# Keeping the turned keys of a head pair between two passes over a batch

## The chip, the cores and the metric

One core of one Trainium2 chip runs the whole program. The metric is the device time of one execution in microseconds (us); every kernel is run several times and the median counts. Engine names as in the profile: PE multiplies matrices, DVE, ACT and POOL work on vectors, SP issues most of the DMAs.

## What is computed

Attention that keeps only the 32 largest scores of each query row, and behind it a channel mix (a gated feed-forward layer) over all heads. Batch 8, 8 heads, 576 positions, head width 64; d_model 512, d_ff 1024.

```python
scores = scale * np.matmul(q, k.transpose(0, 1, 3, 2))
kth = np.partition(scores, -top_k, axis=-1)[..., -top_k:-top_k + 1]
scores = np.where(scores >= kth, scores, -1000000000.0)
attn = np.exp(scores - np.max(scores, axis=-1, keepdims=True))
attn = attn / (np.sum(attn, axis=-1, keepdims=True) + 1e-09)
x = np.matmul(attn, v)            # heads side by side: (batch, 576, 512)
...
xk = mu_k * x + (1.0 - mu_k) * x_prev
xr = mu_r * x + (1.0 - mu_r) * x_prev
k = np.maximum(xk @ w_k, 0.0)
v = k * k @ w_v
r = 1.0 / (1.0 + np.exp(-(xr @ w_r)))
return r * v
```

## The kernel before

**Tiles and visits.** Heads are worked in pairs (`hp`, four pairs a batch). A *visit* is one pair with a part of its query rows: `VISITS` is a list of (batch, pair, part), and `attend` walks it. A part is a range of tiles 0 to 8; tiles 0 to 7 are 64 query rows of both heads (128 partitions), tile 8 is the last 64 rows. A batch is passed over twice, first tiles 0 to 3 of pairs 0, 1, 2, 3, then tiles 4 to 8 of pairs 0, 1, 2, 3; the last batch is passed over three times (0 to 3, 4 to 7, 8). That makes 7 times 8 plus 12, so 68 visits.

**What a visit prepares.** It loads 512 rows of keys of both heads (`load_k`, two DMAs into `kn`), its queries (`qn`), the last 64 key rows (`tl`, and the last 64 query rows where tile 8 belongs to the visit) and the values (`v`). PE turns them with the identity: four transposes for the keys (`turned`, line 834), two for each 256 query rows, one or two for `tl` (line 847); ACT copies each out of PSUM (`K` and `qs` at line 839, `kd` at line 849). Turned keys `K` have two buffers, `kn`, `qn`, `tl` and `v` one each.

**What a tile does.** PE makes scores (889, 885; 876 and 877 for tile 8), ACT copies them to SBUF (894), DVE finds the largest 24 (899, 901, 904), ACT and POOL (919, 921) and DVE (922, 924) find the threshold, ACT exponentiates (927), DVE masks (930), PE turns the result (936, 945), ACT copies it (938, 947), PE multiplies with the values (966, 967), and DVE scales it into `xT` (1001, 1003).

**The channel mix.** `mixes` works `xT` in chunks of 256 rows as soon as their heads are there. PE's matmuls are lines 608 to 610. At the end of a chunk, for each 128 rows, DVE multiplies the matmul's result with the gate in two instructions, `scaled` (line 1137) and `gated` (line 1138), and SP stores the row block (line 1139). `G.l` and `G.e` are SBUF tiles of the gate (`lb`, `eb`), made long before; `pv` is the matmul's result in PSUM (`rot`).

**The flag.** `seen` collects, for every row, whether the fast way to the threshold held; `lowest` (line 1012) reduces it to a column of `least` at the end of each pass. Behind the plan, DVE reduces `least` (1265), PE turns it (1267), DVE reduces and compares (1269, 1271), every engine loads the flag into a register (1272), and a branch (1273) skips the general path, which these inputs never take.

**Order of the work.** Nothing is reordered on the chip: each engine runs its own queue in order. The queues are laid out by `Plan.run`, a list scheduler with a cost and a latency for each operation, which picks the ready operation with the lowest key. A key is the tile number plus a constant of `OFF`; for the mix, a lag behind the tiles it reads. Every operation's place in its queue hangs on all of these constants.

## Time and profile before

| | |
|---|---|
| median of 3 runs | 1284.56 us (1284.15 to 1285.1) |
| the profiled execution | 1283.33 us, of which the span (first to last instruction) is 1281.5 us |
| mean granted clock of PE | 0.986 of full speed |
| instructions | 31120 |

How to read it: the profile divides the span into 40 slices and gives a digit for the busy tenths of each engine. PE and DVE stand at 8 or 9 from the sixth slice to the 36th, and so does ACT; only at the beginning and behind the last attention tile do they part. A share of busy time does not say which of several full engines sets the pace; that is read from the stretches, from the waits, and from the order in which each engine is fed. PE's durations overlap one another, since matmuls are pipelined, so the time that one takes from the queue is read from start to start.

### The profile page before, as it was taken

The page shows a single profiled execution, that of the slowest core. Times are in us where ns is not written, and L with a number is a line of the kernel's source. Part 1 is how long each engine was busy: PE and PEld are TensorE (multiplying, and loading weights), DVE is VectorE, ACT ScalarE, POOL GpSimd, SP SyncE. Part 2 cuts the span into 40 slices and gives each one's busy share as a digit, 9 for nine tenths or more (in the row PEclk, how much of TensorE's full clock was granted, in tenths as well). Part 3 has the DMA queues.
Part 4 walks back from the last instruction along what each step waited for, and adds up shares of the span by engine and source line. Part 5 has one row for each costly group of instructions (what it writes and reads, how often), then busy time and mean ns, then how long its engine had stood idle before and what let it go on. Part 6 is the DMA issues. An engine that isn't in the chain of part 4 may idle for free.

```text
span 1281.5 us, 31120 instructions
## 1 busy us (share of the span) xinstructions
PE 1218.4 (95%) x9349; PEld 935.8 (73%) x9349; DVE 1146.5 (89%) x6228; ACT 1131.4 (88%) x2491; POOL 985.8 (77%) x885
## 2 busy tenths in 40 slices
PE   5876899999999999999999999999999999999996
PEld 2444677777777777777777778777777777777885
DVE  6999999999999999999999999999999989997111
ACT  5998899999999999999999999998989999988441
POOL 2458997978788686978697888786978787878672
PEclk7998999999999999999999999999999999999998
DMA  7144112221221212122312122212222122221100
GB/s 211 40 109 111 47 45 65 48 64 25 57 66 47 59 43 69 40 52 47 78 36 64 25 65 48 65 36 55 48 65 45 47 48 63 48 63 43 32 26 16
DMA packets 218593, 72.51 MB, mean 57 GB/s; under 512 B 211248, under 2 KB 211248, under 8 KB 218416
## 3 DMA queue, kind: packets, MB, share of 16 engines
q1 hardware_dynamic: 217872, 70.31, 22.2%
q8 instruction: 76, 1.25, 0.4%
q14 instruction: 101, 0.83, 0.2%
q10 hardware_dynamic: 544, 0.13, 0.0%
HBM read 60.95 MB, written 9.44 MB: 55 GB/s over the span
## 4 chain that ended last, share of the span: by engine, by line
PE 46%; DVE 25%; ACT 18%; POOL 4%; issue 3%; DMA 2%; SPq 1%; DVEq 0%; ACTq 0%; POOLq 0%
PE rot L608 7%; PE rot L610 7%; PE rot L609 7%; DVE cand L899 7%; PE ps L966 6%; PE rot L936 5%; DVE E L930 5%; PE ps L889 5%; DVE top L922 4%; ACT sc L894 4%; ACT sg L919 3%; ACT se L927 3%; ACT et L938 2%; DVE top L901 2%; DVE cand L904 2%
## 5 line engine op out<-in xcount | busy, mean ns | idle before, releaser
L921 POOL TENSOR_TENSOR sg<-sc,sg 128x576 f32<-128x576 f32 x288 | 409.0, 1424 | 166.7 <-ACT sg L919 164.7
L899 DVE MAX8 cand<-sc 128x8 f32<-128x82 f32 (+1 forms) x2016 | 377.0, 231 | 18.2 <-ACT sc L894 16.3
L919 ACT ACTIVATE sg<-sc,seen 128x576 f32<-128x576 f32 x288 | 226.1, 785 | 13.8 <-DVE seen L911 12.2
L930 DVE SCALAR_TENSOR_TENSOR E<-sc,seen,se 128x576 f32<-128x576 f32 x288 | 231.0, 802 | 0.8 <-issue 0.2
L927 ACT ACTIVATE se<-sc,seen 128x576 f32<-128x576 f32 x288 | 217.5, 755 | 9.9 <-DVE E L930 8.4
L922 DVE MAX8 top<-sg 128x8 f32<-128x576 f32 x288 | 216.0, 750 | 5.9 <-POOL sg L921 5.2
L894 ACT ACTIVATE sc<-ps 128x576 f32<-128x576 f32 x288 | 186.9, 656 | 22.0 <-DVE E L930 8.2
L936 PE MATMUL rot<-ident,E 128*128 128x128 f32 x1152 | 179.6, 279 | 13.7 <-DVE E L930 7.2
L901 DVE MAX8 top<-cand 128x8 f32<-128x56 f32 x864 | 179.2, 208 | 3.8
L608 PE MATMUL rot<-xh,wk 128*128 128x256 f32 (+2 forms) x608 | 180.3, 297 | 0.9 <-ACT ri L994 0.5
L938 ACT ACTIVATE et<-rot 128x512 f32<-128x512 f32 x288 | 174.1, 606 | 7.4 <-PE rot L936 7.1
L936 PEld LDWEIGHTS rot<-ident,E 128*128 128x128 f32 x1152 | 129.9, 141 | 63.9 <-ACT sg L919 7.3
L609 PE MATMUL rot<-xl,wk 128*128 128x256 f32 (+2 forms) x608 | 169.9, 279 | 0.8 <-POOL xl L1087 0.8
L966 PEld LDWEIGHTS ps<-et,v 128*64 128x64 f32 x2560 | 128.5, 137 | 57.0 <-ACT el L947 16.5
L610 PE MATMUL rot<-xh,wk 128*128 128x256 f32 (+2 forms) x608 | 169.8, 279 | 0.0
L966 PE MATMUL ps<-et,v 128*64 128x128 f32 (+1 forms) x2560 | 164.6, 270 | 1.5 <-DVE seen L911 0.5
L889 PE MATMUL ps<-K,qs 64*128 64x512 f32 x512 | 147.4, 653 | 0.0
L608 PE MATMUL rot<-wv,hh 128*128 128x512 f32 (+1 forms) x296 | 127.0, 429 | 0.3 <-ACT qs L839 0.3
L608 PEld LDWEIGHTS rot<-xh,wk 128*128 128x128 f32 x608 | 116.2, 191 | 4.0 <-ACT K L839 1.1
L610 PE MATMUL rot<-wv,hl 128*128 128x512 f32 (+1 forms) x296 | 116.7, 394 | 0.0
L609 PEld LDWEIGHTS rot<-xl,wk 128*128 128x128 f32 x608 | 115.8, 190 | 1.1 <-POOL xl L1087 1.0
L904 DVE MATCH_REPLACE8 cand<-top,cand 128x56 f32<-128x56 f32 x576 | 115.8, 201 | 0.2 <-issue 0.2
(112 smaller groups left out, 2826.9 us busy)
## 6 DMA issues: line engine op xcount, KB each, us to landing
kn<-in_k SPq DMA_DIRECT2D x136, 128.0 KB, 2.5
v<-in_v SPq DMA_DIRECT2D x136, 128.0 KB, 2.5
out<-eb SPq DMA_DIRECT2D x35, 256.0 KB, 2.1
qn<-in_q SPq DMA_DIRECT2D x126, 64.0 KB, 2.2
stage<-in_moe_w_k SPq DMA_DIRECT2D x8, 512.0 KB, 6.0
xT<-in_moe_w_v SPq DMA_DIRECT2D x8, 512.0 KB, 3.6
tl<-in_k SPq DMA_DIRECT2D x136, 16.0 KB, 2.0
vr_in<-in_v SPq DMA_DIRECT2D x128, 16.0 KB, 2.1
```

The source lines that it names most:

```text
L608: nc.tensor.matmul(ps, lhsT=sh, rhs=mh, start=first, stop=False)
L609: nc.tensor.matmul(ps, lhsT=sh, rhs=ml, start=False, stop=False)
L610: nc.tensor.matmul(ps, lhsT=sl, rhs=mh, start=False, stop=last)
L894: return nc.scalar.activation(T.sc.t, sl.t[:, o:o + S], AF.Copy)
L899: lambda T=T, c=c: nc.vector.max(T.cand.t[:, 8 * c:8 * c + 8], T.sc.t[:, CUTS[c]:CUTS[c + 1]]), reads=[T.sc], writes=[(T.cand, c)])
L919: lambda T=T, sn=sn: nc.scalar.activation(T.side.t, T.sc.t, AF.Sign, bias=sn(T, 1), scale=-BELOW, accum_out=T.top.t[:, TOPK:TOPK + 1]),
L921: plan.op(POOL, "below", n, 1375, 1430, lambda T=T: nc.gpsimd.tensor_mul(T.side.t, T.sc.t, T.side.t), reads=[T.sc], writes=[T.side])
L922: plan.op(DVE, "eighth", n, 660, 754, lambda T=T: nc.vector.max(T.top.t[:, 24:32], T.side.t), reads=[T.side], writes=[(T.top, 3)])
L927: plan.op(ACT, "exps", n, 667, 754, lambda T=T, pe=pe, sn=sn: nc.scalar.activation(pe.t, T.sc.t, AF.Exp, bias=sn(T, 0), scale=SCALE), read ...
L930: lambda T=T, U=U, pe=pe, sn=sn: nc.vector.scalar_tensor_tensor(T.e(), T.sc.t, sn(T, 2), pe.t, op0=OP.is_ge, op1=OP.mult, accum_out=U.rs.t ...
L936: nc.tensor.transpose(pt.t[:, c * 128:(c + 1) * 128], E.t[:, o + c * 128:o + (c + 1) * 128], ident)
L966: return [*[nc.tensor.matmul(pa[hs[j]], lhsT=vs[j][:, c, :], rhs=ms[c][j], start=(c == 0), stop=False) for c in range(NKC) for j in range(2)],
```

## The change

**Visits.** The second pass runs over the pairs backwards (3, 2, 1, 0), and two visits of one pair that meet become one. In a usual batch that is 0, 1, 2, 3 (all nine tiles), 2, 1, 0: seven visits in place of eight. In the last batch the third pass runs forwards again, which makes ten in place of twelve; 59 visits in all.

**Turned keys are kept.** `K` has four buffers (`1 + HOLD`). If the same pair comes again within the next six visits, its `K` is put into `held`, and the later visit takes it from there: no load of `kn`, no transposes, no copy. Last key rows (`tl`, `kd`) and values are loaded anew on each visit as before. Queries are loaded in blocks of 256 rows, two for the joined visit, of which the second has a key four tiles later.

**The flag** is made by four operations of the plan (`low`, `lowt`, `lowr`, `lowc`), from one column of `least` for each batch, and the registers are loaded inside the plan's scope.

**The gate.** `scaled` now forms (`G.e` - 2) times `G.l`, both in SBUF, without the matmul's result; `gated` multiplies by -1 and by `pv`.

The planner's constants are new as a whole (`OFF` with about 80 of them, and those below).

```diff
...
-CANDS, BESTS = 0.061, -0.104
-LAG, STEP, WAT, WSTEP, GATE, VALUE, PACE = 11.185, 15.662, 2.065, 0.589, 7.397, 13.484, -2.0
+CANDS, BESTS = 0.045, 0.43
+LAG, STEP, WAT, WSTEP, GATE, VALUE, PACE = 11.262, 15.699, 4.074, 1.023, 7.744, 14.237, -2.0
+HOLD = 3
 HALVES = range(4), range(4, 9)
 EDGE = {B - 1: (range(4), range(4, 8), range(8, 9))}
-VISITS = [(b, hp, part) for b in range(B) for part in EDGE.get(b, HALVES) for hp in range(HP)]
+def visits():
+
+    vs = []
+    for b in range(B):
+        for k, part in enumerate(EDGE.get(b, HALVES)):
+            for hp in range(HP)[::-1] if k % 2 else range(HP):
+                if vs and vs[-1][:2] == (b, hp):
+                    part = range(vs.pop()[2][0], part[-1] + 1)
+                vs.append((b, hp, part))
+                part = EDGE.get(b, HALVES)[k]
+    return vs
+
+
+VISITS = visits()
...
-SLACK = dict(PE=150, ACT=52, DVE=60, POOL=61)
+SLACK = dict(PE=106, ACT=28, DVE=8, POOL=173)
...
-NEAR = dict(PE=151, ACT=168, DVE=28, POOL=268, SP=202)
+NEAR = dict(PE=134, ACT=163, DVE=28, POOL=240, SP=327)
...
-LWAT, LWSTEP = 1.027, 1.455
-LAG0, LAG1 = 10.828, 1.959
+LWAT, LWSTEP = -2.383, 1.423
+LAG0, LAG1 = 9.215, 14.977
...
-MORE = dict(xh=2, xl=2, et=3, top=3, el=1)
+MORE = dict(xh=2, xl=2, et=3, top=3, el=1, K=1 + HOLD)
...
-    least = consts.tile([128, len(VISITS) // HP], F32, name="least")
+    least = consts.tile([128, B + 1], F32, name="least")
+    flag = consts.tile([1, 1], I32, name="flag")
...
-            P.kn, P.tl, P.K, P.kd = buf("kn"), buf("tl"), buf("K"), buf("kd")
-            P.qn, P.qs = (buf("qn"), buf("qs")) if P.first < 8 else (None, None)
-            c0 = P.first // 2
-            nq = sum(1 for i in part if i < 8) // 2
+            P.tl, P.kd, P.K = buf("tl"), buf("kd"), held.pop((b, hp), None)
+            fresh = P.K is None
+            if fresh:
+                P.kn, P.K = buf("kn"), buf("K")
+            if any(x[:2] == (b, hp) for x in visits[p + 1:p + 1 + 2 * HOLD]):
+                held[b, hp] = P.K
+            P.q = {i: (buf("qn"), buf("qs")) for i in part if i % 4 == 0 and i < 8}
             soon = p == 0
 
...
-            plan.op(SP, "kt", at0, 1000, 2700, load_k, writes=[P.kn])
-            if P.qn:
+            if fresh:
+                plan.op(SP, "kt", at0, 1000, 2700, load_k, writes=[P.kn])
+            for i, (qn, _) in P.q.items():
...
+                plan.op(ACT if now else SP, "kq", at0 + i - P.first, 1000, 2700, load_q, writes=[qn])
...
-            turned(P.kn, 4, "k", lambda P=P: P.K.t, P.K)
-            if P.qn:
-                turned(P.qn, nq, "q", lambda P=P, nq=nq: P.qs.t[:, :nq * 128], P.qs, fast=soon)
+            if fresh:
+                turned(P.kn, 4, "k", lambda P=P: P.K.t, P.K)
+            for i, (qn, qs) in P.q.items():
+                turned(qn, 2, "q", lambda qs=qs: qs.t, qs, at0 + i - P.first, fast=soon and i == 0)
...
-            if hp == HP - 1:
-                o = slice(part[0], part[-1] + 1)
-
-                def lowest(s=seen, o=o, m=p // HP):
-                    nc.vector.tensor_reduce(least[:, m:m + 1], s.t[:, :, 1:, o], axis=mybir.AxisListType.XYZ, op=OP.min)
-                plan.op(DVE, "lowest", n, 126, 219, lowest, reads=[seen], writes=[X.least])
+            if p + 1 == len(visits) or visits[p + 1][0] != b:
+                def lowest(s=seen, b=b):
+                    nc.vector.tensor_reduce(least[:, b:b + 1], s.t[:, :, 1:, :], axis=mybir.AxisListType.XYZ, op=OP.min)
+                plan.op(DVE, "lowest", n, 150, 243, lowest, reads=[seen], writes=[X.least])
+        pl = buf("rot")
+        plan.op(DVE, "low", n, 70, 170, lambda: nc.vector.tensor_reduce(least[:, B:], least[:, :B], axis=mybir.AxisListType.X, op=OP.min), writes=[X.least])
+        plan.op(PE_, "lowt", n, 80, 280, lambda: nc.tensor.transpose(pl.t[:1, :128], least[:, B:], ident), reads=[X.least], writes=[pl], mode="T")
+        plan.op(DVE, "lowr", n, 190, 280, lambda: nc.vector.tensor_reduce(least[:1, B:], pl.t[:1, :128], axis=mybir.AxisListType.X, op=OP.min), reads=[pl], writes=[X.least])
+        plan.op(DVE, "lowc", n, 52, 150, lambda: nc.vector.tensor_scalar(flag, least[:1, B:], TINY, None, op0=OP.is_lt), writes=[X.least])
         return xT, ready, starts[-1]
...
-                plan.op(DVE, "scaled", k1, 586, 694, lambda G=G, m=m, pv=pv: nc.vector.scalar_tensor_tensor(pv.t[:m], G.l.t[:m], -1.0, pv.t[:m], op0=OP.mult, op1=OP.mult), reads=[G.l], writes=[pv])
-                plan.op(DVE, "gated", k1, 586, 694, lambda G=G, m=m, pv=pv: nc.vector.scalar_tensor_tensor(G.e.t[:m], G.e.t[:m], 2.0, pv.t[:m], op0=OP.subtract, op1=OP.mult), reads=[pv], writes=[G.e])
+                plan.op(DVE, "scaled", k1, 586, 694, lambda G=G, m=m: nc.vector.scalar_tensor_tensor(G.e.t[:m], G.e.t[:m], 2.0, G.l.t[:m], op0=OP.subtract, op1=OP.mult), reads=[G.l], writes=[G.e])
+                plan.op(DVE, "gated", k1, 586, 694, lambda G=G, m=m, pv=pv: nc.vector.scalar_tensor_tensor(G.e.t[:m], G.e.t[:m], -1.0, pv.t[:m], op0=OP.mult, op1=OP.mult), reads=[pv], writes=[G.e])
...
-        sizes = dict(kn=(1, [128, NKC, 2, D]), qn=(1, [128, NKC, 2, D]), tl=(1, [128, 256]), v=(1, [128, 2, NKC, D]), K=(2, [128, MAIN]), kd=(2, [128, 256]),
-                     qs=(2, [128, MAIN]), sc=(4, [128, S]), cand=(2, [128, 8 * NCH]), top=(4, [128, TOPK + 1]),
+        sizes = dict(kn=(1, [128, NKC, 2, D]), qn=(1, [128, 2, 2, D]), tl=(1, [128, 256]), v=(1, [128, 2, NKC, D]), K=(2, [128, MAIN]), kd=(2, [128, 256]),
+                     qs=(2, [128, 256]), sc=(4, [128, S]), cand=(2, [128, 8 * NCH]), top=(4, [128, TOPK + 1]),
...
+        return nc.values_load(flag, min_val=0, max_val=1)
 
     with ExitStack() as stack:
         stack.enter_context(tc.manual_schedule())
-        pipeline(stack)
-
-    with tc.tile_pool(name="flag", bufs=1) as fp, tc.tile_pool(name="flag_ps", bufs=1, space=PSUM) as fps:
-        low = fp.tile([128, 1], F32, name="low")
-        nc.vector.tensor_reduce(low, least, axis=mybir.AxisListType.X, op=OP.min)
-        row = fps.tile([1, 128], F32, name="row")
-        nc.tensor.transpose(row, low, ident)
-        lowest = fp.tile([1, 1], F32, name="lowest")
-        nc.vector.tensor_reduce(lowest, row, axis=mybir.AxisListType.X, op=OP.min)
-        flag = fp.tile([1, 1], I32, name="flag")
-        nc.vector.tensor_scalar(flag, lowest, TINY, None, op0=OP.is_lt)
-        again = nc.values_load(flag, min_val=0, max_val=1)
+        again = pipeline(stack)
+
...
```

Of the program as built, counted over each engine's queue: PE's transposes of `kn` fall from 272 to 128 and those of `tl` from 100 to 91; ACT's copies to `K` from 68 to 32 and to `kd` (one block) from 36 to 27; SP's loads of `kn` from 136 to 64, of `tl` from keys from 136 to 118, of `v` from 136 to 118, of the values' last rows (`vr_in`) from 128 to 112; DVE's `lowest` from 17 to 8.

PE in the second pass of a batch, before: this is the preparation of a visit with tile 8 (`tl` two blocks), among tiles of the visit ahead (L889, L885 scores, L936, L945 masked tiles).

```order
L847 MATMUL rot_149<-ident,tl_92 128x128 x2
L889 MATMUL ps<-K_94,qs_98 128x512 x2
L885 MATMUL ps<-kd_96,qs_98 128x2x64
L936 MATMUL rot_151<-ident,E_116 128x128 x4
L834 MATMUL rot_149<-ident,kn_90 128x128 x4
L834 MATMUL rot_150<-ident,qn_91 128x128 x2
L945 MATMUL ps<-ident,E_116 128x128
L608 MATMUL rot_151<-xh_130,wk_68 128x256
```

The same place with the change (L856 transposes queries and keys, L870 `tl`, L908 and L912 make scores, L959 and L968 turn masked tiles, L989 multiplies with values).

```order
L990 MATMUL ps<-el_127,vr_in 64x128 x2
L959 MATMUL rot_153<-ident,E_118 128x128 x4
L856 MATMUL rot_154<-ident,qn_92 128x128 x2
L870 MATMUL rot_152<-ident,tl_93 128x128 x2
L959 MATMUL rot_152<-ident,E_118 128x128 x4
L908 MATMUL ps<-kd_99,qs_101 128x2x64
L968 MATMUL ps<-ident,E_118 128x128
L912 MATMUL ps<-K_97,qs_101 128x512 x2
L989 MATMUL ps<-et_124,v_94 64x128
```

The four transposes of the keys are gone; those of the queries and of `tl` remain.

DVE at its queue's end, before: L1137 and L1138 are the last gate blocks, L1265 to L1271 make the flag.

```order
L1137 SCALAR_TENSOR_TENSOR rot_149<-lb_140,rot_149 64x512
L1138 SCALAR_TENSOR_TENSOR eb_137<-eb_137,rot_149 64x512
L1137 SCALAR_TENSOR_TENSOR rot_149<-lb_141,rot_149 128x512
L1138 SCALAR_TENSOR_TENSOR eb_138<-eb_138,rot_149 128x512
L1265 TENSOR_REDUCE low<-least 128x1
L1269 TENSOR_REDUCE lowest<-row 1x1
L1271 TENSOR_SCALAR flag<-lowest 1x1
L1272 TENSOR_LOAD flag
```

With the change, DVE at the end of attention (L947 and L1033 are the last threshold and `lowest`, L1036 to L1039 the flag, L953 masks the last tile, L1163 and L1164 are the gate's two steps).

```order
L947 SCALAR_TENSOR_TENSOR nine_115,seen_117<-se,top_111 128x9
L1033 TENSOR_REDUCE least<-seen_117 128x1
L1036 TENSOR_REDUCE least<-least 128x1
L1038 TENSOR_REDUCE least<-rot_152 1x1
L1039 TENSOR_SCALAR flag<-least 1x1
L1164 SCALAR_TENSOR_TENSOR eb_139<-eb_139,rot_153 64x512
L953 SCALAR_TENSOR_TENSOR E_119,rs_123<-sc_106,seen_117,se 128x576
L996 TENSOR_SCALAR rot_152<-rs_123 128x1
L997 RECIPROCAL rs_123<-rot_152 128x1
L1026 TENSOR_TENSOR xT_146<-ps,ri_128 128x64 x3
L1163 SCALAR_TENSOR_TENSOR eb_140<-eb_140,lb_143 128x512
L1164 SCALAR_TENSOR_TENSOR eb_140<-eb_140,rot_152 128x512
```

The flag now stands ahead of the last mask, and eight more gate instructions follow these rows before DVE loads the flag as the last thing in its queue; SP's load of the flag, which before waited for eight DMA queues, PE and POOL as well, now waits for DVE alone.

## Rows read from the trace of the kernel before

**Rows 1.** page part 1, busy time of each engine
```profile
PE 1218.4 (95%) x9349; PEld 935.8 (73%) x9349; DVE 1146.5 (89%) x6228; ACT 1131.4 (88%) x2491; POOL 985.8 (77%) x885
```

**Rows 2.** stretches of the span, with each engine's busy time
```profile
core 0: us, PE busy (x) PEld busy (x) DVE busy (x) ACT busy (x) POOL busy (x), PEclk, DMA share, GB/s
0.00:200.00 200.00, 157.69 (x990) 102.01 (x991) 185.36 (x887) 169.35 (x356) 133.42 (x124) 0.93 0.35 93
200.00:600.00 400.00, 395.13 (x3193) 307.86 (x3191) 393.80 (x2238) 381.50 (x849) 320.65 (x290) 1.00 0.22 52
600.00:1000.00 400.00, 398.52 (x3166) 310.99 (x3165) 384.74 (x2142) 377.88 (x840) 328.57 (x287) 1.00 0.22 52
1000.00:1180.00 180.00, 177.60 (x1396) 139.72 (x1397) 166.38 (x920) 166.00 (x370) 142.49 (x126) 1.00 0.22 53
1180.00:1281.50 101.50, 89.44 (x610) 75.24 (x609) 16.25 (x46) 36.64 (x81) 60.70 (x62) 0.96 0.09 26
```

**Rows 3.** the same view, of the masking line L930 alone
```profile
200.00:400.00 200.00, 43.19 (x108) 1.00 0.22 52
600.00:1100.00 500.00, 102.28 (x253) 1.00 0.22 53
```

**Rows 4.** timeline of PE: start us, us, instruction
```profile
612.46 0.33 PE L847 MATMUL rot<-ident,tl 128*128 128x128 f32 x1
612.62 0.27 PE L945 MATMUL ps<-ident,E 128*128 128x128 f32 x1
...
613.89 0.65 PE L834 MATMUL rot<-ident,kn 128*128 128x128 f32 x4
614.38 0.39 PE L885 MATMUL ps<-kd,qs 128*128 128x128 f32 x2
```

**Rows 5.** groups: line engine op xcount | busy, mean ns | idle before
```profile
L834 PE MATMUL rot<-ident,kn 128*128 128x128 f32 x272 | 43.8, 286 | 12.5 <-DMA kn<-in_k 10.8 <-ACT et L938 1.4 <-ACT ri L990 0.3
L839 ACT ACTIVATE K<-rot 128x512 f32<-128x512 f32 x68 | 41.1, 605 | 6.1 <-PE rot L834 6.0
```

**Rows 6.** stretch 200 to 1180 us, instructions on the turned keys
```profile
200.00:1180.00 980.00, 152.65 (x492) 41.67 (x492) 34.48 (x57) 1.00 0.22 52
```

**Rows 7.** timeline of the program's end
```profile
1268.71 0.39 PE L609 MATMUL rot<-wv,hh 128*128 128x512 f32 x1
...
1268.94 0.39 PE L610 MATMUL rot<-wv,hl 128*128 128x512 f32 x1
1269.42 0.70 DVE L1137 SCALAR_TENSOR_TENSOR rot<-lb,rot 128x512 f32<-128x512 f32 x1 [17.47 <-PE rot L610]
1270.22 0.69 DVE L1138 SCALAR_TENSOR_TENSOR eb<-eb,rot 128x512 f32<-128x512 f32 x1
1270.94 0.33 SPq L1139 DMA_DIRECT2D out<-eb  x1
1273.22 0.17 DVE L1265 TENSOR_REDUCE low<-least 128x1 f32<-128x17 f32 x1 [2.31 <-DMA out<-eb]
...
1274.22 0.14 DVE L1271 TENSOR_SCALAR flag<-lowest 1x1 int32<-1x1 f32 x1
```

**Rows 8.** source lines behind the flag: count, duration ns min/median/max, first and last start
```profile
L1272 PEldq TENSOR_LOAD <-flag x1: 488/488/488, 1274.6 to 1274.6; - x1
...
L1273 PEldq COMPARE_BRANCH  x1: 3882/3882/3882, 1275.2 to 1275.2; - x1
...
L1336 SPq EVENT_SEMAPHORE  x10: 17/28/28, 1280.2 to 1281.5; - x10
```

**Rows 9.** groups of POOL's product and of the first gate step
```profile
L921 POOL TENSOR_TENSOR sg<-sc,sg 128x576 f32<-128x576 f32 x288 | 409.0, 1424 | 166.7 <-ACT sg L919 164.7
...
L1137 DVE SCALAR_TENSOR_TENSOR rot<-lb,rot 128x512 f32<-128x512 f32 (+1 forms) x37 | 25.4, 686 | 67.9 <-PE rot L610 67.8
```

**Rows 10.** waits of DVE behind 1180 us: us, times, longest
```profile
DVE rot L1137 <- PE rot L610: 67.8, 7, 20.2
```

**Rows 11.** waits of PE ahead of 200 us: us, times, longest
```profile
PE rot L834 <- DMA kn<-in_k: 9.7, 3, 4.7
```

More of the change, by code (lines that the diff above doesn't have):

```diff
@@ L46 @@
-CANDS, BESTS = 0.061, -0.104
-LAG, STEP, WAT, WSTEP, GATE, VALUE, PACE = 11.185, 15.662, 2.065, 0.589, 7.397, 13.484, -2.0
+OFF = dict(kt=-24.682, kq=-9.775, rest=-13.394, v=-5.073, v8=8.399, tk=-5.088, ck=-3.016, tq=-4.466, cq=-5.729, tr=-0.99, cr=-8.985, zero=26.741,
+           score=-0.305, score8=-16.363, keep=-0.702, cand=5.175, best=-6.77, drop=-17.414, under=-0.972, nb=6.314, count=2.406, below=-0.034,
+           eighth=5.4, nine=7.048, exps=3.042, mask=2.258, turn=3.521, et=4.406, turnl=4.279, el=0.332, weigh=1.23, inv=6.6, inv2=-0.753,
+           turni=-5.161, ri=4.56, place=-1.898, lowest=11.386, ranks=1.008, mu=-8.732, nmu=20.632, changek=16.045, sharek=6.336, addk=-15.444,
+           xhk=3.381, xlk=-26.53, changer=-11.566, sharer=8.77, addr=10.933, xhr=5.939, xlr=-9.1, hidden=1.376, relu=-3.776, sq=2.602, r2=6.527,
+           hl=-6.961, gate=1.635, gexp=2.338, ga=11.247, ln=3.288, inv1=4.629, newton=-11.796, value=-0.174, scaled=-9.381, gated=-4.072,
+           store=12.146, w=18.924, wabs=-4.306, wclamp=0.885, wshift=-9.236, wsign=0.581, wexp=-1.85, wfine=2.14, whi=8.188, wmul=10.013,
+           wsub=-10.654, wlo=1.658, spread=1.602, sliver=-7.978, low=3.66, lowt=-12.415, lowr=-14.586, lowc=-1.397)
```

38 lines of the change are left out of this document (15 added, 23 removed).

## The prediction

> **What bounds the kernel now.** I read the page's busy times first, then stretches of the span, then the timeline of single places, and the program's end last. The page alone decides nothing: PE is busy 95% of the span, DVE 89%, ACT 88% [rows 1]. The stretches say more [rows 2]. In the first 200 us PE lies idle for 42.3 us (200 less 157.69); DVE is the full engine there. From 200 to 1180 us PE is busy for 395.13 + 398.52 + 177.60 = 971.3 of 980 us, so it is idle for 8.7 us, at the full granted clock (1.00, the level of 2.4 GHz). DVE is busy for 944.9 us of the same 980 and idle for 35.1. Behind 1180 us DVE has almost nothing left, and PE works off mix matmuls that have piled up, until its last one starts at 1268.94 us [rows 7]. So PE's queue is full from 200 us to its end: whatever leaves that queue should bring the end nearer by the time that it took. DVE is a near second. From 200 to 400 us it masks 54 tiles (108 records of line L930, two for each tile, one of them the accumulator's read), which is 27.0 in 100 us; from 600 to 1100 us it masks 126.5, which is 25.3 [rows 3]. DVE can go faster than it does in the later stretch, and what holds it there is PE.
>
> **Keys no longer turned.** One turn of a pair's keys is four transposes. In the timeline the first of the four starts at 613.89 us and what comes behind them at 614.38, so a turn takes 0.49 us of PE's queue; one transpose of `tl` takes 612.62 less 612.46, 0.16 us [rows 4]. I use start to start, since a listed duration (0.65 and 0.33 us) overlaps the next instruction. The change drops 36 of 68 turns and 9 transposes of `tl`. Of the 68 copies to `K` [rows 5], 57 lie between 200 and 1180 us [rows 6]; the eleven ahead are the eight visits of batch 0 and three of batch 1. Batch 0 loses four turns and one `tl`, in the stretch where PE has 42 us to spare, and I count those 2.1 us at nothing; DVE's work covers them, and if DVE did not fill that stretch they would count in full. That leaves 32 x 0.49 + 8 x 0.16 = 15.7 + 1.3 = **17.0 us** off a full queue. Bounds: nothing, if DVE sets the pace in its place, and 32 x 0.65 + 8 x 0.33 = 23.4 us, if the whole durations went. I take 17.0, because the start-to-start gap is what a full queue gives back.
>
> **Their copies and loads.** ACT loses 36 copies of 605 ns [rows 5], 21.8 us. ACT is busy for 925.4 of the 980 us [rows 2], so it is not the last to be free, and I count this at nothing; it shortens waits behind ACT, which is one reason why the range reaches further down than the sum. SP issues 72 key loads fewer, and fewer of values and last rows. Of PE's waits for key loads, 10.8 us in all [rows 5], 9.7 lie ahead of 200 us [rows 11]; behind it 1.1 us could go, and I count nothing. One load moves: the joined visit's second query block comes four tiles later in SP's queue, behind the loads of its neighbours. There are eight of these; if each made PE wait like the one key load behind 200 us (1.1 us), that would be 9 us lost. The block has four tiles of time, some 16 us at 25.3 tiles in 100 us, so I take nothing and keep the 9 us for the range.
>
> **Gate multiplied out early.** The number of DVE instructions stays. The first, 686 ns [rows 9], no longer waits for the last matmul; only the second stands behind it. In the middle that is worth nothing, as no store is urgent and the PSUM buffer comes free one DVE step sooner. The new first step reads two SBUF tiles; no row shows such an instruction on DVE, for both steps of before read the matmul's PSUM tile. Nearest rows: 0.69 us at the lower end; at the upper end it also waits out one POOL product, 1.42 us more [rows 9]. I take 0.69, since it has the same 512 elements as the rows nearest to it, and keep the other end for a rival.
>
> The Trainium skill speaks against this step (GPSIMD Engine Reference, Key points): GpSimd shares its SBUF interfaces with VectorE, and DVE instructions with two SBUF inputs contend with it. No row here tests that; by it the sum would lie between mine and that of the rival on two SBUF tiles below.
>
> **The flag.** In the plan it adds a wait: DVE's second reduction waits for PE's transpose, with the last mask and the last products for `xT` queued behind it. In before, with PE free, the chain runs from 1273.22 to 1274.22, so the wait is below 1 us; with six mix matmuls ahead of it, 0.23 us each by their starts, some 1.4 us more [rows 7]. The PE queue is full with mix work at that time [rows 2], so a late mask costs nothing; without that backlog it would cost about 2 us.
>
> At the end the steps run one behind the other [rows 7, 8]: last matmul done at 1269.33, first gate step at 1269.42, second at 1270.22, store at 1270.94, landed and seen at 1273.22, flag ready at 1274.36, then PE's register load (0.49) and its branch (3.88 us from 1275.2), and 2.4 us from the branch's end to the span's end, 1281.5. That is 12.2 us behind the last matmul. With the change every register load waits for the flag alone, which is long made. PE can begin at 1269.33: 1269.33 + 0.49 + 3.88 = 1273.7. Beside that, one gate step (to 1270.1) and the store (2.28 us from issue to DVE's start) are over at 1272.4. So PE's branch is later, and 1273.7 + 2.4 = 1276.1: **5.4 us** less. Bounds: 1.9 us, if the registers still come behind the store and only one gate step (0.80) and the flag's own chain (1.14) go; 6.7 us, if PE's branch no longer takes its 3.88 us and the store sets the end (1272.4 + 2.4 = 1274.8). I take 5.4, as it uses each row as it stands.
>
> **Sum.** 17.0 + 5.4 = 22.4 us. The profiled execution took 1283.33 us, 1.83 beyond its span; less 22.4 that is 1260.9. The median of before is 1284.56, 1.23 above the profiled execution, so I forecast 1262.2. Does DVE allow it? It has 944.9 us to do in 980 - 17.0 = 963 us, 98.1%. From 200 to 600 us it is busy for 393.80 of 400, 98.5% [rows 2]. It fits, with little room.
>
> **Rivals.**
>
> *DVE takes over as the bound.* For it: 98.1% is close to the most that DVE shows anywhere, and its queue is in order, so each late input costs. Against it: its 25.3 tiles in 100 us where PE is fullest, beside 27.0. If DVE gained nothing, only the end's 5.4 us would be left, 1279.2; if it allowed half of the 17.0, the time is 1270.7, and I take that as this case's centre.
>
> *The start gains too.* Of the 9.7 us that PE waits for keys there [rows 11], the longest wait, 4.7 us, is the first load of the program as I read it; the other 5.0 and the 2.1 us of turns could go: 1262.2 - 7.1 = 1255.1. Against it: DVE, not PE, fills that stretch.
>
> *Two SBUF tiles hold up DVE (slower).* Of 37 gate blocks seven lie behind 1180 us [rows 10], so 30 fall into DVE's full stretch. If each new first step takes x us more, DVE needs (944.9 + 30x) / 0.985 us; with the end's 5.4 us given back this passes 980 from x = 0.86. With a full POOL product each, x = 1.42, it needs 1002.6 us: 1284.56 + 22.6 - 5.4 = 1301.8. For it: POOL is busy 77% [rows 1]. Against it: a wait for POOL would be for what is left of a product, about half of 1.42.
>
> *The keys are kept, but the new order loses what they give.* Every constant of the planner is new, so PE may wait where it did not. That the keys are not kept after all is excluded: the built queues hold 128 of these transposes in place of 272. A loss of 17 to 22 us is needed for no change; nothing in the rows points to it.
>
> **How the numbers follow.** About 0.2% (2.6 us) is what a measurement of this kernel can tell from no change. Forecast 62% (1256 to 1267), DVE as the bound 18% (1267 to 1279), a better start 12% (1250 to 1256), two SBUF tiles 5%, order loses it 3%. The range 1252 to 1275 holds the forecast, most of the better start, and the larger part of DVE's case; the 9 us of query loads end inside it, at 1271. Faster by over 0.2%: 92%; within: 3%; slower: 5%.
>
> **What would show it.** Right: between 200 us and the last attention tile PE is still idle for no more than some 10 us and DVE at 98% or more; that stretch is shorter by about 17 us; the last matmul stands 6.8 us before the span's end in place of 12.2. Wrong: PE waits behind DVE for tens of us (DVE as the bound); the first gate step's mean is 1.5 us or more, or DVE stands idle ahead of it (two SBUF tiles); PE's branch is short or stands behind the store (the end's term).

## The result, and the profile after

The changed kernel takes 1301.95 us (median of 4 runs, 1300.73 to 1303.52), the kernel before 1284.36 beside it: a ratio of **1.0139 [1.0121, 1.0156]**. It is 17.6 us slower, where 22 us less were forecast. The profiled execution's span is 1298.8 us.

The page's part 1 of the changed kernel, to be laid beside [rows 1]:

```profile
PE 1217.8 (94%) x9196; PEld 922.0 (71%) x9196; DVE 1168.6 (90%) x6219; ACT 1116.2 (86%) x2446; POOL 994.4 (77%) x885
```

PE has fewer instructions, as the kept keys would have it, but is busy for as long; DVE has about as many as before (6219 beside 6228) and is busy for 22 us more. The stretches, to be laid beside [rows 2], show where PE's room went:

```profile
core 0: us, PE busy (x) PEld busy (x) DVE busy (x) ACT busy (x) POOL busy (x), PEclk, DMA share, GB/s
0.00:200.00 200.00, 156.65 (x956) 102.61 (x957) 183.19 (x877) 163.61 (x341) 131.13 (x120) 0.91 0.30 84
200.00:600.00 400.00, 385.35 (x3073) 294.73 (x3072) 391.78 (x2193) 370.12 (x819) 314.70 (x284) 1.00 0.17 42
600.00:1000.00 400.00, 389.61 (x3038) 298.21 (x3037) 383.51 (x2093) 364.73 (x804) 323.04 (x280) 1.00 0.17 41
1000.00:1180.00 180.00, 176.30 (x1377) 136.24 (x1375) 173.37 (x930) 160.72 (x360) 144.33 (x126) 1.00 0.15 38
1180.00:1298.80 118.80, 109.89 (x761) 90.21 (x759) 36.76 (x132) 56.97 (x127) 81.22 (x78) 0.99 0.10 26
```

From 200 to 1180 us PE is now busy for 385.35 + 389.61 + 176.30 = 951.3 us and idle for 28.7 (8.7 before). DVE is busy for 948.7 of the same 980 (944.9 before), and yet it is 20 us behind: past 1180 us it still has 36.76 us to do, where before it had 16.25. The granted clock is 1.00 in all of these 980 us, before and after, so the clock is no part of the answer there. The chain that ended last, by engine, has turned round. Of the kernel before:

```profile
PE 46%; DVE 25%; ACT 18%; POOL 4%; issue 3%; DMA 2%; SPq 1%; DVEq 0%; ACTq 0%; POOLq 0%
```

and of the changed one:

```profile
DVE 48%; PE 26%; ACT 13%; POOL 5%; issue 4%; DMA 1%; SPq 1%; POOLq 0%; ACTq 0%; DVEq 0%
```

**The gate's first step** is the first thing on DVE that differs. Groups of DVE by line (line, engine, operation, count, then busy us and mean ns); L1163 is the first step, [rows 9] has it for before:

```profile
L1163 DVE SCALAR_TENSOR_TENSOR eb<-eb,lb 128x512 f32<-128x512 f32 (+1 forms) x37 | 42.3, 1143 | 56.6 <-POOL eb L1152 56.6
...
L1164 DVE SCALAR_TENSOR_TENSOR eb<-eb,rot 128x512 f32<-128x512 f32 (+1 forms) x37 | 24.9, 674 | 4.6 <-PE rot L627 4.3
```

Both steps read 128x512 elements. The second reads one SBUF tile and the matmul's PSUM tile and takes 674 ns; the first reads two SBUF tiles and takes 1143 on average, against 686 before, which adds 16.9 us to its group (42.3 less 25.4). Another group of DVE is listed with more time for the same work, the search for the largest in each part of a row (before, then the change):

```profile
L899 DVE MAX8 cand<-sc 128x8 f32<-128x82 f32 (+1 forms) x2016 | 377.0, 231 | 18.2 <-ACT sc L894 16.3
...
L922 DVE MAX8 cand<-sc 128x8 f32<-128x82 f32 (+1 forms) x2016 | 401.2, 232 | 14.9 <-ACT sc L917 14.5 <-issue 0.2
```

2016 times 231 ns would be 466 us, so DVE's listed durations overlap one another too, and in the change they overlap less. DVE's busy time is therefore no exact measure of its work either. For the first gate step, the view of its source line gives the spread (ns, min/median/max):

```profile
L1163 DVE SCALAR_TENSOR_TENSOR eb<-eb,lb x37: 667/1154/1903, 174.9 to 1291.4; 128x512 f32<-128x512 f32 x35, 64x512 f32<-64x512 f32 x2
```

The shortest is as fast as before, the longest nearly three times as long. What makes the difference stands beside it in the timeline, on POOL:

```profile
337.23 1.42 POOL L944 TENSOR_TENSOR sg<-sc,sg 128x576 f32<-128x576 f32 x1 [0.67 <-ACT sg L942]
337.58 1.61 DVE L1163 SCALAR_TENSOR_TENSOR eb<-eb,lb 128x512 f32<-128x512 f32 x1
338.60 1.75 POOL L1152 TENSOR_TENSOR eb<-eb,lb 128x512 f32<-128x512 f32 x1
...
547.35 1.92 POOL L1149 TENSOR_SCALAR eb<-eb 128x512 f32<-128x512 f32 x1
547.82 0.69 DVE L1163 SCALAR_TENSOR_TENSOR eb<-eb,lb 128x512 f32<-128x512 f32 x1
...
1196.09 1.27 POOL L1152 TENSOR_TENSOR eb<-eb,lb 128x512 f32<-128x512 f32 x1
1197.33 1.42 POOL L944 TENSOR_TENSOR sg<-sc,sg 128x576 f32<-128x576 f32 x1
1197.40 1.90 DVE L1163 SCALAR_TENSOR_TENSOR eb<-eb,lb 128x512 f32<-128x512 f32 x1 [1.51 <-POOL eb L1152]
```

At 1197.40 us POOL's product has 1.35 us left (until 1198.75), and DVE's step ends 0.55 us behind it, at 1199.30. At 337.58 us the product has 1.07 us left (until 338.65), and the step ends at 339.19, 0.54 behind it. So DVE waits until POOL's product is over and then does the rest of its own work. These two are not picked out: 24 of the 37 first steps begin while a POOL product with a row of its own is under way, and each of them ends 0.54 to 0.60 us behind that product. The wait doesn't stand in the view of waits, since it lies within the instruction's listed time. POOL pays too: its next product, begun at 338.60 us, takes 1.75 us where the same line takes 1.27 at 1196.09. Beside POOL's `TENSOR_SCALAR`, which has one input tile, DVE's step at 547.82 us takes its plain 0.69 us.

**The end**, to be laid beside [rows 7, 8], in the timeline of the changed kernel:

```profile
1290.04 1.29 POOL L1152 TENSOR_TENSOR eb<-eb,lb 128x512 f32<-128x512 f32 x1 [1.48 <-ACT lb L1151]
...
1290.98 0.39 PE L627 MATMUL rot<-wv,hl 128*128 128x512 f32 x1
1291.36 0.69 DVE L1163 SCALAR_TENSOR_TENSOR eb<-eb,lb 128x512 f32<-128x512 f32 x1 [18.20 <-POOL eb L1152]
1292.15 0.69 DVE L1164 SCALAR_TENSOR_TENSOR eb<-eb,rot 128x512 f32<-128x512 f32 x1
1292.87 0.33 SPq L1165 DMA_DIRECT2D out<-eb  x1
```

and in the views of the two lines behind the plan, the register load (L1284) and the branch (L1290):

```profile
L1284 PEldq TENSOR_LOAD <-flag x1: 489/489/489, 1287.2 to 1287.2; - x1
L1284 SPq TENSOR_LOAD <-flag x1: 508/508/508, 1293.3 to 1293.3; - x1
L1290 SPq EVENT_SEMAPHORE  x8: 17/17/17, 1296.9 to 1297.4; - x8
L1290 PEldq COMPARE_BRANCH  x1: 3355/3355/3355, 1287.7 to 1287.7; - x1
L1290 SPq COMPARE_BRANCH  x1: 50/50/50, 1294.2 to 1294.2; - x1
```

From the last matmul's end (1291.37) to the span's end are 7.4 us, where there were 12.2. PE's branch, 3.4 us long, begins at 1287.7 on the sequencer, ahead of PE's last matmuls, and is hidden behind them; both gate steps, the store and SP's own load of the flag set the end. The first gate step no longer needs the matmul, but it has to wait for POOL's product `eb` (1290.04 to 1291.33 us), which ends only 0.04 us before the last matmul does. For the last block the gate's tile is not made long before; it was as late in the kernel before:

```profile
1267.99 1.28 POOL L1126 TENSOR_TENSOR eb<-eb,lb 128x512 f32<-128x512 f32 x1 [1.48 <-ACT lb L1125]
```

There it ended at 1269.27 us, 0.06 us before the last matmul.

### The profile page after: what moved, and what is told of

Same layout as the page of the kernel before. It is cut to its first block, busy times and chain, and to the rows that moved or that the text cites. A ratio compares the mean times of both kernels' runs of the same rounds, so it can differ in the third digit from the quotient of the medians.

```text
span 1298.8 us, 30461 instructions
## 1 busy us (share of the span) xinstructions
PE 1217.8 (94%) x9196; PEld 922.0 (71%) x9196; DVE 1168.6 (90%) x6219; ACT 1116.2 (86%) x2446; POOL 994.4 (77%) x885
## 3 DMA queue, kind: packets, MB, share of 16 engines
q1 hardware_dynamic: 167632, 57.95, 17.6%
## 4 chain that ended last, share of the span: by engine, by line
DVE 48%; PE 26%; ACT 13%; POOL 5%; issue 4%; DMA 1%; SPq 1%; POOLq 0%; ACTq 0%; DVEq 0%
DVE cand L922 12%; DVE E L953 9%; DVE top L945 8%; DVE top L924 5%; PE rot L625 5%; DVE cand L927 5%; PE rot L627 4%; PE rot L626 4%; PE ps L989 3%; ACT sg L942 3%; ACT sc L917 3%; PE rot L959 2%; ACT se L950 2%; PE ps L912 2%; DVE nine L947 2%
## 5 line engine op out<-in xcount | busy, mean ns | idle before, releaser
L922 DVE MAX8 cand<-sc 128x8 f32<-128x82 f32 (+1 forms) x2016 | 401.2, 232 | 14.9 <-ACT sc L917 14.5
L953 DVE SCALAR_TENSOR_TENSOR E<-sc,seen,se 128x576 f32<-128x576 f32 x288 | 231.3, 803 | 2.0 <-ACT se L950 0.8
L950 ACT ACTIVATE se<-sc,seen 128x576 f32<-128x576 f32 x288 | 216.4, 751 | 16.6 <-DVE E L953 12.0
L945 DVE MAX8 top<-sg 128x8 f32<-128x576 f32 x288 | 215.4, 748 | 5.4 <-POOL sg L944 4.8
L959 PE MATMUL rot<-ident,E 128*128 128x128 f32 x1152 | 180.0, 279 | 24.4 <-DVE E L953 11.3
L917 ACT ACTIVATE sc<-ps 128x576 f32<-128x576 f32 x288 | 181.7, 651 | 23.4 <-DVE E L953 6.3
L959 PEld LDWEIGHTS rot<-ident,E 128*128 128x128 f32 x1152 | 130.9, 142 | 72.4 <-ACT sg L942 15.1
L989 PE MATMUL ps<-et,v 128*64 128x128 f32 (+1 forms) x2560 | 167.2, 272 | 4.9 <-DMA v<-in_v 1.3
L989 PEld LDWEIGHTS ps<-et,v 128*64 128x64 f32 x2560 | 130.6, 139 | 56.7 <-issue 20.9
L912 PE MATMUL ps<-K,qs 64*128 64x512 f32 x512 | 149.7, 662 | 0.3 <-ACT sc L917 0.2
L625 PE MATMUL rot<-wv,hh 128*128 128x512 f32 (+1 forms) x296 | 126.9, 429 | 1.5 <-DVE eb L1164 0.8
L626 PE MATMUL rot<-wv,hh 128*128 128x512 f32 (+1 forms) x296 | 115.9, 392 | 0.0
```

Of the source, the lines that this page charges most:

```text
L625: nc.tensor.matmul(ps, lhsT=sh, rhs=mh, start=first, stop=False)
L626: nc.tensor.matmul(ps, lhsT=sh, rhs=ml, start=False, stop=False)
L922: lambda T=T, c=c: nc.vector.max(T.cand.t[:, 8 * c:8 * c + 8], T.sc.t[:, CUTS[c]:CUTS[c + 1]]), reads=[T.sc], writes=[(T.cand, c)])
L945: plan.op(DVE, "eighth", n, 660, 754, lambda T=T: nc.vector.max(T.top.t[:, 24:32], T.side.t), reads=[T.side], writes=[(T.top, 3)])
L950: plan.op(ACT, "exps", n, 667, 754, lambda T=T, pe=pe, sn=sn: nc.scalar.activation(pe.t, T.sc.t, AF.Exp, bias=sn(T, 0), scale=SCALE), read ...
L953: lambda T=T, U=U, pe=pe, sn=sn: nc.vector.scalar_tensor_tensor(T.e(), T.sc.t, sn(T, 2), pe.t, op0=OP.is_ge, op1=OP.mult, accum_out=U.rs.t ...
```

## The experiments

The first theory behind them: the gate's first step, and a new planner constant for DVE, make DVE late. The rivals: the turned keys are worth less than their time on PE, the new visits cost something, or any new plan differs from the next. "Same order" below means that every engine's queue holds its instructions in the order of the kernel named, but for those left out or exchanged; "planned anew" means that all queues were laid out again. The edits are shown in short, with arguments and lines left out. Times are medians in us; ratios stand against the kernel before, run beside each. Beside the different runs it took 1282.6 to 1284.4, so a difference between two runs that were not made side by side is good to about 1 us.

### The gate alone, in the order of before

```diff
-"scaled": scalar_tensor_tensor(pv, G.l, -1.0, pv, op0=mult, op1=mult)
-"gated": scalar_tensor_tensor(G.e, G.e, 2.0, pv, op0=subtract, op1=mult)
+"scaled": scalar_tensor_tensor(G.e, G.e, 2.0, G.l, op0=subtract, op1=mult)
+"gated": scalar_tensor_tensor(G.e, G.e, -1.0, pv, op0=mult, op1=mult)
```

> The kernel before with the change's two gate formulas at the old places: every engine's queue keeps its order, and only the operands of 37 DVE instructions differ (the first step reads two SBUF tiles, the second the matmul's result). Theory A (two SBUF tiles on DVE collide with POOL and lengthen a queue that sets the pace): the first step's mean rises from 686 to 1000 ns or more, and the time by 8 to 14 us, to 1292 to 1298 us. Theory B (the new order of the work, not the gate, costs the time): no more than 4 us from 1284.4.

Measured: 1292.54, ratio 1.0073 [1.0056, 1.009]; 9.9 us more than before. The group of the first step in this run:

```profile
L1137 DVE SCALAR_TENSOR_TENSOR eb<-eb,lb 128x512 f32<-128x512 f32 (+1 forms) x37 | 37.3, 1009 | 54.5 <-POOL eb L1126 54.5
```

37 times 1009 less 686 ns [rows 9] is 12.0 us of DVE's listed time, beside 9.9 us at the end. POOL pays about as much: it is busy for 997.0 us in this run, where it was for 985.8 [rows 1].

```profile
PE 1224.9 (95%) x9349; PEld 935.8 (72%) x9349; DVE 1156.7 (90%) x6228; ACT 1131.3 (88%) x2491; POOL 997.0 (77%) x885
```

Whether DVE's delay or POOL's is what reaches the end, no run here separates. The same collision, in another order, has another mean: it hangs on where POOL's products happen to lie.

### The change without its second SBUF tile, same order

The first step multiplies with a constant 1.0 that lies in PSUM (256 columns, read twice); it leaves out the factor `G.l`.

```diff
-scalar_tensor_tensor(G.e, G.e, 2.0, G.l, op0=subtract, op1=mult)
+scalar_tensor_tensor(G.e, G.e, 2.0, X.ones, op0=subtract, op1=mult)
```

> The changed kernel with every queue in its order, but the first gate step multiplies by a constant of 1.0 in PSUM in place of the SBUF tile: it leaves out the factor G.l, so the output is not the reference's. One small instruction more at the start. Theory A: the step's mean falls from 1150 to about 690 ns and the time by 10 to 16 us, to 1286 to 1292 us. Theory B: no more than 4 us from 1302.

Measured: 1293.41, ratio 1.0077 [1.006, 1.0094]; 8.5 us less than the change. The same line of the changed kernel, now with one tile in PSUM (`se` is PSUM):

```profile
L1163 DVE SCALAR_TENSOR_TENSOR eb<-eb,se x37: 667/680/689, 177.2 to 1284.5; 128x512 f32<-128x512 f32 x35, 64x512 f32<-64x512 f32 x2
```

The spread is gone, and with it 8.5 us. With the run before it, that shows the gate's term from both sides. It was less than expected, though: some 11 us above before are left, with the keys kept and a shorter end.

### The keys' relief alone, in the order of before

Later passes load, turn and copy no keys, and their scores use what lies in the buffer. Of the edit, the turn:

```diff
...
-turned(P.kn, 4, "k", lambda P=P: P.K.t, P.K)
+turned(P.kn, 4, "k", lambda P=P: P.K.t, P.K, skip=P.first >= 4)
...
```

> The kernel before with every queue in its old order, less the key loads, the 144 key transposes and the 36 copies of the later passes: scores there use whatever keys lie in the buffer, so the output is not the reference's. My prediction's step (PE's queue sets the pace, each dropped turn gives back 0.49 us): 17 us less, 1264 to 1270 us. Rival (DVE sets the pace as soon as PE is relieved): at most 5 us less, 1279 us or more.

Measured: 1276.15, ratio 0.9946 [0.993, 0.9963]; 6.5 us less, not 17. The stretch from 200 to 1180 us of this run (the columns are those of [rows 2]):

```profile
200.00:1180.00 980.00, 967.64 (x7669) 749.58 (x7668) 946.18 (x5315) 916.35 (x2032) 797.13 (x707) 1.00 0.18 44
```

PE has 83 matmuls fewer in that time than before (7669 against 3193 + 3166 + 1396 = 7752), and still counts as busy for 967.6 us of 980. Over the whole span, the turns' listed time falls from 43.8 us [rows 5] to 21.0, PE's busy time only from 1218.4 [rows 1] to 1210.1:

```profile
PE 1210.1 (95%) x9205; PEld 922.0 (72%) x9205; DVE 1143.5 (90%) x6228; ACT 1116.7 (88%) x2455; POOL 985.1 (77%) x885
...
L834 PE MATMUL rot<-ident,kn 128*128 128x128 f32 x128 | 21.0, 290 | 9.7 <-DMA kn<-in_k 9.7
```

So 22.8 listed us are gone and 8.3 busy us. Listed durations overlap, and those of other matmuls grew (L889 from 653 to 660 ns each); PE's busy share does not say how much its queue has to do.

### Keys turned on every visit of the new order

```diff
-if any(x[:2] == (b, hp) for x in visits[p + 1:p + 1 + 2 * HOLD]):
+if False:
```

> The changed kernel, planned anew, with keys turned on each of the 59 visits (27 turns more than the change has): the same constants, visits, gate and flag. If PE's queue is what a turn costs: 27 x 0.49 = 13 us more, 1311 to 1319 us. If DVE sets the pace, or if a new plan is worth more than the turns: no more than 6 us from 1302, on either side.

Measured: 1315.73, ratio 1.0256 [1.0239, 1.0274]; planned anew, 13.8 us more than the change, as the view of PE's queue had it (13). But this is one new plan against another, and plans of one program differ by as much for other reasons (below), so it does not show what the keys give in the new order.

### Old constants, and the old gate, under the new visits

One run gives the change all constants and the gate of before, the other the old gate alone; both are planned anew.

> The change's visits, kept keys and flag, with the old gate and all the old constants of the planner. Theory C (what loses beside the gate is the order that the new constants make): the kept keys give what they gave in the old order (6.5 us) and the flag what the end of the changed kernel shows (4.7 us), so 1268 to 1276 us. Rival D (the visits that run backwards, or keys held over several visits, lose by themselves): 1280 us or more.

Measured: 1285.8, ratio 1.0015 [1.0001, 1.0029]. No gain, from keys and flag together. That is rival D's time; a later plan of the same visits speaks against D (the last experiment).

> The changed kernel with the old gate, its new constants kept, planned anew. From the run with the constant in PSUM: 8.5 us less than the change, 1290 to 1297 us. If more than 4 us away from that, a new plan by itself moves the time by that much.

Measured: 1285.39, ratio 1.001 [0.9997, 1.0023]; 16.6 us less than the change, where the gate's step gives 8.5 at a fixed order. The rest came with the new plan.

### The planner's slack for DVE

```diff
-SLACK = dict(PE=106, ACT=28, DVE=8, POOL=173)
+SLACK = dict(PE=106, ACT=28, DVE=60, POOL=173)
```

> The changed kernel with one constant of the planner put back: the slack that it adds to DVE's wait for a result, 60 in place of 8. In the built queue, DVE instructions that stand directly behind the one whose result they read fall from 328 to 250 (before: 261). Theory C1 (such neighbours stall DVE, and DVE sets the pace): 6 to 10 us less, 1291 to 1297 us. Rival (DVE is not what loses): within 4 us of 1302.

Measured: 1289.01, ratio 1.0038 [1.0025, 1.0051]; 13 us less than the change. And the other way round, before with 8 in place of 60:

> The kernel before with that one constant as in the change, 8 in place of 60, planned anew: such neighbours rise from 261 to 324. Theory C1: 6 to 10 us more, 1289 to 1294 us. Rival: within 4 us of 1283.5.

Measured: 1306.17, ratio 1.0166 [1.0139, 1.0194]; 23 us more than before. Both went the way expected, and further than the 6 to 10 us. Taken by themselves they looked like a second cause, the constant 8.

### DVE's relief, alone and with PE's, in the order of before

```diff
-"scaled": lambda: nc.vector.scalar_tensor_tensor(pv, G.l, -1.0, pv, ...)
+"scaled": lambda: None
```

> The kernel before, same order on every engine, without the gate's first step (37 VectorE instructions of 0.69 us, some 32 of them while attention runs): leaves out the factor 1/(1+exp) of the gate. If VectorE's queue sets the pace together with its waits: 8 to 17 us less than before, 1266 to 1275. If PE's queue alone sets it: at most 4 us less, 1279 or more.

Measured: 1280.27, ratio 0.9978 [0.9968, 0.9987]; 3.0 us less, for 25.4 us of DVE's time [rows 9]. DVE's queue doesn't set the pace. The number is in the range that was written for PE's queue alone, but that view had already failed in the run with fewer turns (6.5 of 17.0 us). From 200 to 1180 us, and the busy times of the whole span:

```profile
200.00:1180.00 980.00, 972.71 (x7769) 761.52 (x7768) 934.73 (x5283) 926.97 (x2064) 794.49 (x705) 1.00 0.22 52
...
PE 1221.6 (95%) x9349; PEld 939.1 (73%) x9349; DVE 1127.6 (88%) x6191; ACT 1129.5 (88%) x2491; POOL 985.5 (77%) x885
```

DVE is idle for 45.3 us in the stretch, where it was for 35.1 [rows 2], and for 151.6 us of the whole span (1279.2 less 1127.6), where it was for 135.0: most of what was taken out came back as waits.

> The kernel before, same order, with both taken out: the later passes' key loads, turns and copies (these passes use stale keys) and the gate's first step (the factor 1/(1+exp) is left out). If PE and VectorE hold each other (either one's relief is capped by the other), this gains more than the two single runs together: over 6.5 us plus what the gate's step alone gave. If VectorE alone sets the pace, it gains about what the gate's step gave, plus at most 6.5 us; if PE alone, 6.5 us and no more than 4 on top.

Measured: 1274.14, ratio 0.9924 [0.9908, 0.9939]; 9.1 us less, about the 6.5 + 3.0 of the two single runs. So PE and DVE don't hold each other either: freed together, they gain no more than one by one. The sum fits both other views of the expectation as well, so this run says no more than that. In this order, less than half of what is taken out of a queue comes off the time: 6.5 of 17.0 us for PE, 3.0 of 25.4 for DVE.

### All the change's parts, in the order of before

Keys are kept in four tiles of their own, and the flag is made behind the last `place`; visits, constants and order are those of before.

```diff
+P.keys = X.keys[(HP * b + hp) % len(X.keys)]
...
+if o.name == "place" and places == 96:
+    make_flag()
...
-pipeline(stack)
+again = pipeline(stack)
```

> The kernel before with its own visits, constants, gate and order on every engine, and two of the change's parts put in by hand: the turned keys stay in four tiles of their own, one per head pair, from a batch's first pass to its later ones (no load, no turn, no copy in later passes), and the flag is made right behind the last placed output and loaded ahead of the end. Theory (VectorE with its waits sets the pace, so the keys are worth what the run with fewer turns gave, 6 to 7 us, and the tail 3 to 5 us): 1270 to 1275 us. The prediction's own view (PE's queue is the pace, 17.0 + 5.4 us): 1258 to 1264. If the keys' new tiles or the flag inside the program cost something that the run with fewer turns didn't show: 1277 or more.

Measured: 1274.92, ratio **0.994 [0.9927, 0.9954]**. This beats both kernels, and leaves nothing out. In its trace the end is that of the change (the register load of PE stands at L1275, the branch at L1281):

```profile
L1281 PEldq COMPARE_BRANCH  x1: 3572/3572/3572, 1261.6 to 1261.6; - x1
```

while its last matmul starts at 1264.99 us, 4 us earlier than before. With the change's gate on top (the edit of the first experiment):

> The kernel before's order on every engine with all three parts of the change put in by hand: keys kept, flag inside, and the change's gate formulas. If the parts add at a fixed order: the run with keys and flag (1274.9) plus the gate's 8.5 to 9.9, 1283 to 1286, and what the change has above that (16 to 19 us) is its new plan and its visits. If the parts themselves collide (keys kept leave less room to hide the gate): 1290 or more. If the gate is hidden once PE has room: 1280 or less.

Measured: 1286.1, ratio 1.0022 [1.0013, 1.0031]; 11.2 us more than without it.

```profile
L1141 DVE SCALAR_TENSOR_TENSOR eb<-eb,lb 128x512 f32<-128x512 f32 (+1 forms) x37 | 37.0, 1000 | 53.0 <-POOL eb L1130 53.0
```

The parts add up in a fixed order. What the change has beyond them, 1301.95 less 1286.1, **15.9 us** (some 15 by the ratios), lies in the new visits and the new plan.

### Is it the constant, or the plan?

Four more values of DVE's slack, each planned anew: 50 and 72 in before, 20 and 45 in the change.

> The kernel before with the planner's VectorE slack at 50 in place of 60; all engines are planned anew. If the slack's size is what counts: within 5 us of before (1278 to 1288). If plans scatter by themselves: 1289 or more, for the constants of before were fitted together and any other plan is worse.

Measured: 1291.98, ratio 1.0071 [1.0048, 1.0094].

> The kernel before with the planner's VectorE slack at 72 in place of 60; all engines are planned anew. If the slack's size is what counts: within 5 us of before (1278 to 1288). If plans scatter by themselves: 1289 or more.

Measured: 1298.17, ratio 1.0114 [1.0095, 1.0134].

> The change with the planner's VectorE slack at 20 in place of 8. If the slack's size is what counts: between the change (1302.0) and the run at 60 (1289.0), some 1297 to 1300. If plans scatter: anywhere from 1289 to 1315, and above 1304 it would speak against the size.

Measured: 1291.06, ratio 1.0061 [1.0044, 1.0078].

> The change with the planner's VectorE slack at 45 in place of 8. If the slack's size is what counts: near the run at 60 (1289.0), some 1287 to 1294, and under the run at 20. If plans scatter: no order between 8, 20, 45 and 60.

Measured: 1295.9, ratio 1.0097 [1.008, 1.0114].

| slack of DVE | 8 | 20 | 45 | 50 | 60 | 72 |
|---|---|---|---|---|---|---|
| before | 1306.2 | | | 1292.0 | 1283.5 | 1298.2 |
| the change | 1302.0 | 1291.1 | 1295.9 | | 1289.0 | |

The theory of the constant's size falls: in the change 20 is faster than 45, and in before 50 and 72, close to the old value, are 8.5 and 14.7 us slower than 60. With this one constant changed, all queues are laid out anew, and the plans differ by up to 13 us in the change and 23 us in before, in no order that the constant's size would tell; 8 is the slowest of four in both rows, and more than that two draws don't show. The neighbours on DVE of the two runs above were not counted for these four, so what they cost stays open. The four plans of before have a mean of 1294.9 us, those of the change 1294.5. So the kernel before has the fastest of its four plans, the change the slowest of its four, and a comparison of the two compares plans as much as parts.

The traces show two ways in which a plan loses. With slack 72, DVE of the kernel before is busy for 1145.9 us, no more than before (1146.5), so on DVE the whole loss is waiting; from 200 to 1180 us the wait that grew is that for POOL's `sg` (us, times, longest; before, then slack 72):

```profile
DVE top L922 <- POOL sg L921: 4.1, 9, 1.0
...
DVE top L922 <- POOL sg L921: 18.1, 20, 3.2
```

The change, beside the run with all its parts in the old order, has DVE busy for 1168.6 us where that run has 1156.1, which is 12.5 of the 15.2 us between their spans. The gate's first step takes 5.3 us more of it (42.3 and 37.0), and the search overlaps less in the change (401.2 us, above) than in that run:

```profile
L903 DVE MAX8 cand<-sc 128x8 f32<-128x82 f32 (+1 forms) x2016 | 375.5, 230 | 16.9 <-ACT sc L898 15.6 <-issue 0.2
```

That this is what costs the time is not shown: the change with slack 20 has 403.1 us there and is 10.9 us faster.

### The change with old gate and slack 60

> The change with two things taken back: the gate's old formulas, and the planner's VectorE slack of 60 in place of 8; reversed passes, kept keys and the flag stay. If the slack of 8 and the gate are two separate causes, this lies about 10 us under the run with the slack alone at 60 (1289.0) and 8 to 13 us under the run with the old gate alone (1285.4): 1274 to 1280. If both act on the same slack of VectorE's queue and don't add: 1283 to 1289. A new plan by itself can move some us either way. Under 1272 this would beat every other version of the change.

Measured: 1274.75, ratio **0.9932 [0.9918, 0.9945]**, as fast as the version in the order of before (1274.92). With reversed visits, kept keys, flag and old gate there are now three plans: 1285.8, 1285.4 and 1274.75. So the new visits need not cost anything; how much of the 15.9 us is theirs in the change's own plan is not shown.

## Why the prediction was wrong

**PE's queue as the pace: failed.** The step is "whatever leaves that queue should bring the end nearer by the time that it took". Its term of 17.0 us measured 6.5 with nothing else changed. The 971 busy us of 980 were read as a full engine; but with the turns gone PE was listed as busy for nearly as long, in the same stretch and with fewer instructions. The Trainium skill (Perfetto Trace Analysis, Identifying the Most-Contended Engine) says that the busy share of matmuls is no good measure of how near PE is to its limit, and points to the busy share of the weight loads. Here these stand at 758.6 of 980 us, 77% [rows 2], and the runs agree as far as PE goes: most of what was taken out of its queue did not shorten the run. By that section of the Trainium skill DVE, whose busy share counts as it stands, would be the engine to relieve first, at 96%; there the measurement differs, for 25.4 us taken from DVE gave 3.0, and DVE's durations overlap as well (466 us of one group listed in 377.0). What paces attention in this order is neither PE's queue nor DVE's by itself; ACT's and POOL's were not relieved alone. It isn't settled further than that: the chain from tile to tile through PE, ACT, POOL and DVE, each in its own order, may be what does, and no run here took one link of it out.

**The first gate step at 0.69 us: failed.** It measured 1.14 us on average in the change, and cost 8.5 to 11.2 us of time in three pairs at a fixed order. The mechanism is that of the rival on two SBUF tiles, with about a third of a product per step (0.46 us more on average; a whole one, 1.42, was priced, and half of one named as likely). The sign that was to show it, a mean of 1.5 us, was set too high. The rival's time, 1301.8, was met by accident: it let the collision begin to cost only from 0.86 us a step on, since DVE was thought to have room until 98.5%. In truth 0.32 us a step (1009 less 686 ns) already cost 9.9 us. DVE in the change is at 948.7 of 980 us, 96.8%, and at 97.9% in its fullest stretch. The three pairs say what the collision costs in a fixed order, beside the time that it adds to DVE's step: 9.9 us for 12.0 in the order of before, 11.2 for 11.6 (37 times 1000 less 686 ns) with the keys kept, 8.5 for 17.1 (37 times 1143 less 680 ns) in the order of the change. POOL's busy time grew as well, by 10.7 to 11.2 us in the three pairs, so not all of the cost need be DVE's. What is taken off DVE alone counts for far less, 3.0 of 25.4. A reading that fits, and that no run tested: the order was laid out around the old durations, so that a late instruction hands its delay on and an early one only waits for the next input.

**The plan: the rival with 3% cost no less than the other two misses.** "Nothing in the rows points to it" was true, and no evidence: rows of one plan cannot show what another plan costs. 15.9 us of the miss (some 15 by the ratios) lie in the plan and the new visits together, beside 14 us that keys and flag didn't give and 11 for the gate. The likeliest case was given a width of 11 us, where four plans of one and the same program lie 23 us apart.

**The flag: the size nearly right, the path not.** The end took 12.2 us behind the last matmul and takes 7.4, so 4.7 us less; 5.4 were forecast. The forecast put PE's register load and branch there. But PE's branch doesn't wait for PE's last matmul, and so falls out of the path; both gate steps, the store, and SP's load and branch behind it stand there in its place. The first gate step was to be gone from the end, and is not, since POOL's product for it ends only 0.04 us before the last matmul. That the sum came near is partly luck.

**Loads, copies, the moved query blocks: counted at nothing, and not told apart.** The run with fewer turns drops the turns, their loads and their copies, and all three together gave 6.5 us; how much of it each gave is not shown. The query blocks were not tried by themselves.

In one sum: 1283.2 before, less 8.3 for kept keys and flag, plus 11.2 for the gate, plus 15.9 for visits and plan, is 1302.0.

## What to carry to other kernels

That an engine is listed as 99% busy does not show that it is the bound; that work taken off it shortens the run does. So take the work off, in the same order, before believing the sum. Before an operand is moved from PSUM to SBUF on DVE, look at what POOL does beside it: with two SBUF inputs it waited out POOL's product here, and the view of waits did not show it. Where a planner lays out the queues, compare parts of a change in one fixed order, and compare plans over several draws; a single new plan can be worth more than the change.

## What was not expected of the hardware

DVE's wait for POOL is one for the whole instruction, not a slowing of both. In each of the two collisions shown, DVE's step ended 0.54 and 0.55 us behind the end of the POOL product that was under way when it began, and a POOL product that came second took 1.75 us in place of 1.27. The Trainium skill (SBUF — State Buffer, Who interferes with whom) agrees: such a DVE instruction contends with a GpSimd instruction that reads SBUF, and it calls the ports that the two share an exclusive lock. The traces differ in one point. POOL's `TENSOR_SCALAR` at 547.35 us reads an SBUF tile as well, and DVE's step beside it took 0.69 us; of the two other steps that began during this instruction, one took 0.69 and one 0.81 us, and both were over 0.58 us or more before it ended. Beside a shorter `TENSOR_SCALAR` (L1003, 0.41 us from 1076.98 us) the step took 0.75 us and ended 0.54 us behind it. What sets the two apart is not shown.

PE's branch takes 3.4 to 4.8 us over the runs, those of the other engines 45 to 76 ns in the change; where its flag is ready early, as in the change, PE's sequencer begins it ahead of PE's last matmuls (1287.7 us, the last matmul at 1290.98), and it no longer sets the end.
